# A linear-attention layer feeding a routed expert layer on one core: fourth and fifth chunk routed sooner, early fetches at once, breaks between indirect DMAs

## The chip, the cores and the metric

One core of one Trainium2 chip runs the whole kernel. The metric is device time in microseconds (us) for one execution. Three runs of the kernel before took 639.36, 640.45 and 640.35 us; their median is 640.35 us. The profile is of one further execution.

## The reference

Attention over B = 4 batches, H = 8 heads, S = 768 positions, head width D = 48: per position `state = f * state + outer(k, v)` with `f = sigmoid(f_logit)`, and `y = q @ state`. The result is laid out as x with N = 3072 rows of 384. Then a noisy top-2 router sends every row to two of eight experts:

```python
logits = x @ w_gate
noise_scale = np.log1p(np.exp(x @ w_noise))
noisy_logits = logits + noise_scale * noise
top2 = np.argpartition(-noisy_logits, 2, axis=1)[:, :2]
...
h = np.maximum(x[mask] @ w1[e], 0.0)
out[mask] += top2_w[mask, k, None] * (h @ w2[e])
```

`w1[e]` is 384 x 1024 and `w2[e]` is 1024 x 384; `top2_w` is the softmax of the two winning logits.

## The kernel before, in words

**Attention.** The 768 positions are six chunks of 128 (`NCH = 6`, `HALF = 3`). A chunk of all four batches is worked through in two groups, so there are twelve groups (`NG = 12`); groups 2c and 2c+1 make chunk c. A group turns q and k into transposed form on TensorE (L563), multiplies them (`scores`, `sc`, L584), masks the product on VectorE (`A`, L587), multiplies it with v (L615) and adds the share of the older state (L621). The state is carried on by GpSimd (`mid`, `st`, L604 and L606). The output yT is turned back for storing (`xp`, L632) and multiplied with the router's weights (`lt`, L642, and `lp`, L651).

**The order.** Everything up to the end of the attention is written out by hand: a loop over i runs the generators `back(i)` and `front(i)` (L1642 to L1689), and each name they yield ("sc0", "y1", "f" and so on) is a slot. In a slot the loop gives the router one step (three once the fifth chunk is being routed), lets at most one waiting scatter go (`puts.pop(0)()`), and gives one step to `first_loads` (L1517). After slot "L0" (or "f" in the groups without one) of every second i the next chunk's `route(c)` is started. In each engine's queue instructions run in the order in which they are written.

**Routing.** `route(c)` (L659) takes a chunk's logits to noisy logits, finds the two best (L681, L682), the gates (L686 to L694), counts per expert (L699 to L711), ranks the rows by two products on TensorE (`rk`, L716 and L717) and from these computes each row's place in its expert's list (`sloti`, L727). Then eight `put` steps each issue one indirect DMA on GpSimd (L731) that scatters 32-byte entries into the DRAM table `lists`. Behind each stands a memset (L739): one element of `spacer`, or, in the first three chunks at every third put, one row of 2048 elements of `spare`, which is a part of `hs_a`. This long memset is called a break below.

**Early pairs.** A pair is 256 rows of one expert. When three chunks are in the lists (24 puts), `first_loads` waits eight slots, fetches the row numbers of pairs 0 and 1 (`slots<-lists`, L864, issued by SyncE, SP), and gathers their x rows with four indirect DMAs on GpSimd (`xg<-x_rows`, L878). At the end of the attention they are turned on TensorE (`xgp`, L930) and give items 0 and 1, 256 rows each of two experts: first layer L983, second layer L1255. The eight puts of each later chunk stand behind the gathers, with a `spacer` each. When all six chunks are in the lists the remaining pairs are fetched, gathered and multiplied (L1145, L1311), and outputs are scattered onto the result by GpSimd (L1192).

Of the kernel before, what the change touches and what calls it, by code (L numbers as in the profile page):

```python
# [11 lines left out]
F32 = mybir.dt.float32  # L12
# [320 lines left out]
def kernel(  # L333
# [38 lines left out]
    nc = tc.nc  # L372
    B, H, S, D = q.shape
    N, DM = out.shape
# [3 lines left out]
    NCH = S // C  # L378
# [6 lines left out]
    HALF = NCH // 2  # L385
    NP = 3 * E
    NI = 2 * E
    NE = 2
# [270 lines left out]
    def route(c):  # L659
# [48 lines left out]
        else:  # L708
# [1 line left out]
        upto[c] = t([E, B + 1], "upto")  # L710
        nc.vector.tensor_tensor_scan(upto[c].rearrange("t e b -> t (e b)"), data0=carry.rearrange("t e b -> t (e b)"),  # L711
                                     data1=each.rearrange("t e b -> t (e b)"), initial=0.0, op0=ALU.mult, op1=ALU.add)
        for _ in range((4, 5, 5, 5, 8, 8)[c]):
            yield from pause()
        rk = one_bank(f"rk_{c}")[:, 0:B * E].rearrange("t (e b) -> t e b", b=B)
        nc.tensor.matmul(rk, lhsT=earlier, rhs=each[:, :, 1:], start=True, stop=False)  # L716
# [12 lines left out]
        def put(b, r):  # L729
            n_put.append(c)  # L730
            into = nc.gpsimd.indirect_dma_start(  # L731
                out=lists, out_offset=bass.IndirectOffsetOnAxis(ap=sloti[:, r, b:b + 1], axis=0),
                in_=entry[:, c, b, r, :], in_offset=None)
            tc.declare_no_dep(into.ins, group="lists", reason="slots differ")
            tc.add_to_no_dep_group("lists", into.ins)
            if c >= HALF:
                tc.declare_no_dep(into.ins, group="full", reason="slots differ")
                tc.add_to_no_dep_group("later", into.ins)
            nc.gpsimd.memset(spare[0:1, :] if c < HALF and len(n_put) % 3 == 0 else spacer, 0.0)  # L739

        puts.extend([partial(put, b, r) for b in range(B) for r in range(2)])
        yield


    steer_q = []

# [125 lines left out]

    def gather(p, halves=(0, 1)):

        if 0 in halves:
            xg[p] = moved.tile([128, 2, DM], F32, tag="xg", name=f"xg{p}", bufs=4)
        for s in halves:
            nc.gpsimd.indirect_dma_start(out=xg[p][:, s, :], out_offset=None, in_=x_rows[0:HALF * B * C] if p < NE else x_rows,  # L878
                                         in_offset=bass.IndirectOffsetOnAxis(ap=slots[p][:, s, 0:1], axis=0))

    def stored(p):
        if in_blocks(p):
# [634 lines left out]
    def first_loads():  # L1517
        while n_routed < HALF or len(n_put) < HALF * B * 2:
            yield
        for _ in range(8):  # L1520
            yield
        for what, p, pause in (("fetch", 2, 4), ("first", 0, 0), ("second", 0, 2), ("first", 1, 0), ("second", 1, 2), ("fetch", 3, 0)):
            if what == "fetch":
                ahead(what, p)
            elif what == "first":
                gather(p, (0,))
            elif what == "second":
                gather(p, (1,))
                done["gather"] = p + 1
            for _ in range(pause):  # L1530
                yield

    def tables():
# [12 lines left out]
    def through(g):  # L1546
        return 0 <= g < NG

    def front(i):
        if through(i + 1):  # L1550
            for s in range(2):
                turn_q(i + 1, s)
                yield f"q{s}"
            if i >= 0:
                load("q", i + 3)
                load("k", i + 3)
            for s in range(2):
                turn_k(i + 1, s)
                yield f"k{s}"
        if i == NG - 1:  # L1560
            turned_logits(i - 1)
            logits(i)
            features(i)
            turned_logits(i)
            yield "L0"
            yield "x0"
            yield "x1"
        else:
            yield "x0"
            if through(i):  # L1570
                features(i)
            yield "x1"
            if through(i - 1):
                turned_logits(i - 1)
        if i == -1:
            forget(1)
        elif through(i + 2):
            for s in range(2):
                summed(i + 2, s)
                yield f"L{s}"  # L1580
            ends(i + 2)
            if i == -2:
                for nm, g in (("f", 2), ("v", 1), ("q", 2), ("k", 2)):
                    load(nm, g)
            load("f", i + 5)
        if i == -3 or i > 2:
            forget(i + 3, halves if i < 0 else whole)
        yield "f"

    def back(i):  # L1590
# [39 lines left out]
        if i == -1:  # L1630
            scaled(0, halves)
        if through(i):
            yield "y1"
            for s in range(2):
                if i:
                    before(i, s, old)
                yield f"st{s}"
# [4 lines left out]
    for i in range(-3, NG):  # L1642
        for what in chain(back(i), front(i)):
# [16 lines left out]
                part_of_weights(n_part // 8, 1 + n_part // 4 % 2, n_part % 4)  # L1660
            elif i == NG - 1 and what in ("x0", "x1", "f"):
                zeros(4)
            for _ in range(6 if n_routed == NCH else 3 if n_routed == NCH - 1 else 1):
                next(router, None)
            slot += 1
            if puts and (what in ("q1", "x1", "L1", "sc1", "lg", "y1") + ("k1", "ds") * (n_routed == HALF) if n_routed < NCH - 1 else True) and not (done["fetch"] and not done["gather"]):
                puts.pop(0)()
            next(first_pairs, None)
            if i == NG - 1 and what == "st1":
# [3 lines left out]
            if what in fill.get(i, ()):  # L1673
# [4 lines left out]
                if what == "f":  # L1678
                    for _ in range(6):
                        next(router, None)  # L1680
            if what == ("L0" if through(i + 2) or i == NG - 1 else "f") and (i >= 2 and i % 2 == 0 or i == NG - 1):
                c = (i - 1) // 2
                router = chain(router, route(c))
                n_routed = c + 1
# [96 lines left out]
```

## Time and profile before

| what | value |
|---|---|
| median of three runs | 640.35 us |
| profiled execution, its own time | 634.29 us |
| span in that profile | 632.6 us |
| mean granted TensorE clock | 0.982 of full speed |
| TensorE matmul busy | 606.6 us, 96% |
| VectorE, ScalarE, GpSimd busy | 459.8, 279.8, 238.6 us |

The profiled execution took 6.06 us less than the median of the three runs, and its span lies 1.7 us below its own time. Times below are from the span's start. Attention ends at about 157 us; items 0 and 1 run to some 190 us, and the later items fill the rest. A granted clock of 1.00 is the full 2.4 GHz, 0.50 is 1.2 GHz.

### The profile page before, as it was taken

To read this page: it belongs to the slowest core of one execution; us is meant where nothing else is said; L and a number is where in the kernel's file an instruction comes from. 1 tells how busy PE (TensorE), PEld (TensorE's weight loads), DVE (VectorE), ACT (ScalarE), POOL (GpSimd) and SP (SyncE) were. 2 spreads that over 40 slices of the span, in tenths; PEclk is the share of its full clock that TensorE was granted. 3 is DMA by queue.
4 is the path that set the end of the run, shared out by engine and by line. 5 is a ranking of instruction groups with operands and counts; after the bars stand their busy time and mean duration, and the time that the engine had idled before them with its cause. 6 is when DMAs were issued, how large, how long until landed. Compare 5 with 4: busy or idle time off the path is not lost.

```text
span 632.6 us, 12895 instructions
## 1 busy us (share of the span) xinstructions
PE 606.6 (96%) x4767; PEld 543.4 (86%) x4767; DVE 459.8 (73%) x1031; ACT 279.8 (44%) x715; POOL 238.6 (38%) x250
## 2 busy tenths in 40 slices
PE   8999999878979999999999999999999999999995
PEld 7888878666969899998899899889888988898995
DVE  6658877745656675897797888787777978887850
ACT  5766665612113332327524731662175137316621
POOL 3213598861854513160134314322431262232032
PEclk9999999996989999999999999999999999999998
DMA  9999998885334667859576976688587849541024
GB/s 195 187 201 195 215 220 194 209 255 184 129 98 131 143 145 177 204 91 276 144 180 137 281 188 145 165 240 188 142 258 162 206 105 285 175 68 23 0 26 55
DMA packets 184511, 104.71 MB, mean 166 GB/s; under 512 B 144284, under 2 KB 177564, under 8 KB 184440
## 3 DMA queue, kind: packets, MB, share of 16 engines
q1 hardware_dynamic: 172392, 84.46, 52.3%
q0 software_dynamic: 12048, 19.35, 16.8%
q8 instruction: 39, 0.64, 0.4%
q14 instruction: 32, 0.26, 0.1%
HBM read 76.80 MB, written 27.23 MB: 164 GB/s over the span
## 4 chain that ended last, share of the span: by engine, by line
PE 88%; DVE 5%; issue 3%; another core or an unknown queue 2%; ACT 1%; DMA 1%; POOL 0%; POOLq 0%; DVEq 0%; ACTq 0%
PE y L1311 28%; PE D L1145 6%; PE E L1145 6%; PE C L1145 5%; PE B L1145 5%; PE sc L615 4%; PE sc L584 4%; PE hp L983 3%; PE y L1255 2%; PE L L541 2%; PE qp L563 2%; PE kp L563 2%; PE sc L621 2%; PE ds L596 2%
## 5 line engine op out<-in xcount | busy, mean ns | idle before, releaser
L1192 POOL DMA_INDIRECT out_dram<-ys,slots x48 | 79.7, 1661 | 192.2 <-DVE ys L1317 128.0
L1311 PE MATMUL y<-q_all,f_all 128*128 128x192 f32 x528 | 94.8, 327 | 0.8 <-ACT ys L1327 0.8
L1311 PEld LDWEIGHTS y<-q_all,f_all 128*128 128x128 f32 x528 | 86.6, 190 | 1.6 <-ACT ys L1327 1.3
L878 POOL DMA_INDIRECT xg<-x_rows,slots x48 | 52.2, 1087 | 71.5 <-DMA slots<-lists 28.2
L1311 PE MATMUL y<-w,hs_b 128*128 128x192 f32 x352 | 64.4, 326 | 0.0
L731 POOL DMA_INDIRECT lists<-entry,sloti x48 | 49.7, 1036 | 32.0 <-DVE sp L675 12.7
L1311 PEld LDWEIGHTS y<-w,hs_b 128*128 128x128 f32 x352 | 58.4, 190 | 0.4
L1317 DVE SCALAR_TENSOR_TENSOR ys<-y,slots,ys 128x192 f32<-128x192 f32 x66 | 27.4, 415 | 43.0 <-PE y L1311 16.5
L1153 ACT ACTIVATE hs_b<-hs_b 128x256 f32<-128x256 f32 x120 | 50.2, 418 | 8.5 <-DVE hs_b L1157 6.6
L1360 ACT ACTIVATE ys<-y,slots 128x192 f32<-128x192 f32 x22 | 9.2, 420 | 100.8 <-PE y L1311 100.8
L587 DVE TENSOR_TENSOR A<-sc,causal 128x1024 f32<-128x1024 f32 x24 | 28.6, 1220 | 16.9 <-PE sc L584 11.4
L584 PEld LDWEIGHTS sc<-qT,kT 64*128 64x128 f32 x384 | 24.3, 199 | 13.2 <-issue 8.4
L584 PE MATMUL sc<-qT,kT 64*128 64x128 f32 x384 | 27.3, 292 | 6.9 <-issue 3.8
L1311 PE MATMUL y<-w,f_all 128*128 128x192 f32 x176 | 32.7, 329 | 0.0
L1311 PE MATMUL y<-q_all,hs_b 128*128 128x192 f32 x176 | 32.7, 329 | 0.0
L1311 PEld LDWEIGHTS y<-q_all,hs_b 128*128 128x128 f32 x176 | 28.9, 190 | 2.1 <-issue 2.1
L1180 DVE TENSOR_TENSOR f_all<-hs_b 128x512 f32<-128x512 f32 x44 | 29.9, 684 | 0.0
L1311 PEld LDWEIGHTS y<-w,f_all 128*128 128x128 f32 x176 | 28.9, 190 | 0.8
L615 PEld LDWEIGHTS sc<-A,v_all 128*64 128x64 f32 x384 | 22.6, 144 | 7.4 <-issue 3.8
L1145 PE MATMUL C<-v_all,ws_b 128*128 128x256 f32 x96 | 28.7, 380 | 0.1
L615 PE MATMUL sc<-A,v_all 128*64 128x128 f32 x384 | 26.9, 289 | 1.5 <-issue 1.2
L1150 ACT COPY hs_a<-D 128x256 f32<-128x256 f32 x66 | 24.4, 370 | 7.2 <-PE D L1145 5.4
(274 smaller groups left out, 1410.5 us busy)
## 6 DMA issues: line engine op xcount, KB each, us to landing
w<-in_moe_w_dram SPq DMA_DIRECT2D x40, 384.0 KB
w_q<-in_moe_w_dram SPq DMA_DIRECT2D x10, 1536.0 KB
w<-in_moe_w_dram SPq DMA_DIRECT2D x6, 1536.0 KB
rows_of<-xg SPq DMA_DIRECT2D x18, 384.0 KB
v_all<-in_v_dram SPq DMA_DIRECT2D x12, 384.0 KB
x_rows<-xs SPq DMA_DIRECT2D x12, 384.0 KB
out_dram<-zero SPq DMA_DIRECT2D x24, 192.0 KB
k_all<-rows_of SPq DMA_DIRECT2D x48, 96.0 KB
```

Of the source, the lines that this page charges most:

```text
L563: nc.tensor.transpose(to[:, cols(hp)], flat[:, cols(hp)], ident)
L584: nc.tensor.matmul(sc[:, par, cols(hp)], lhsT=kT[g][rows(par), s, cols(hp)], rhs=qT[g][rows(par), s, cols(hp)], start=True, stop=True)
L587: nc.vector.tensor_tensor(A[g, s].rearrange("j r (a i) -> j (r a) i", i=C), sc.rearrange("j r (a i) -> j (r a) i", i=C), causal.unsqueeze( ...
L615: nc.tensor.matmul(at(g, s, h), lhsT=slot_of("v", g)[:, s, h, :], rhs=A[g, s][:, h % 2, cols(h // 2)], start=(j < 2), stop=(g < 2 and j >= ...
L731: into = nc.gpsimd.indirect_dma_start(out=lists, out_offset=bass.IndirectOffsetOnAxis(ap=sloti[:, r, b:b + 1], axis=0), in_=entry[:, c, b, ...
L878: nc.gpsimd.indirect_dma_start(out=xg[p][:, s, :], out_offset=None, in_=x_rows[0:HALF * B * C] if p < NE else x_rows, in_offset=bass.Indir ...
L1145: nc.tensor.matmul(banks[name, j], lhsT=half_of(x, k)[:, j * 128:(j + 1) * 128], rhs=half_of(y, k), start=first, stop=True, skip_group_che ...
L1153: nc.scalar.activation(at(to, j), at(y, j), AF.Relu, scale=-1.0 if more[0][0] == "-" else 1.0)
L1180: nc.vector.tensor_tensor(sm[which], x, y, op)
L1192: into = nc.gpsimd.indirect_dma_start(out=out, out_offset=bass.IndirectOffsetOnAxis(ap=slots[p][:, s, 2:3], axis=0), in_=ys[s], in_offset= ...
L1311: nc.tensor.matmul(to, lhsT=x[:, o, :], rhs=y[:, o, :], start=(start and o == 0), stop=(o == FH - 1), skip_group_check=not start)
L1317: nc.vector.scalar_tensor_tensor(to, in0=bank, scalar=gate[s], in1=to, op0=ALU.mult, op1=ALU.add)
```

## The change

The pauses in `route` and the steps per slot are altered, so that the fourth and the fifth chunk's places are known earlier; the fifth chunk's routing starts at "y1" of i = 10, and the logits it needs are moved ahead of that. `first_loads` waits two slots in place of eight, and then until four puts of the fourth chunk are out. Puts may now go in any slot once the fourth chunk is being routed. A new function `breath` counts indirect DMAs in a row, puts and early gathers alike, and makes every third one's memset a break: the old one for the first 24 puts, and after that two memsets in a row, of 768 and 576 elements, on one row of a tile (`xg[2]`) that is not in use yet. The sixth chunk's eight puts keep the spacer.

```diff
-        for _ in range((4, 5, 5, 5, 8, 8)[c]):
+        for _ in range((4, 5, 5, 17, 11, 8)[c]):
             yield from pause()
...
-            nc.gpsimd.memset(spare[0:1, :] if c < HALF and len(n_put) % 3 == 0 else spacer, 0.0)
+            breath(c <= HALF + 1)
...
+    in_a_row = [0]
+
+    def breath(broken):
+        in_a_row[0] = (in_a_row[0] + 1) % 3
+        if in_a_row[0] or not broken:
+            nc.gpsimd.memset(spacer, 0.0)
+        elif len(n_put) <= HALF * B * 2:
+            nc.gpsimd.memset(spare[0:1, :], 0.0)
+        else:
+            if NE not in xg:
+                xg[NE] = moved.tile([128, 2, DM], F32, tag="xg", name=f"xg{NE}", bufs=4)
+            flat = xg[NE].rearrange("p s w -> p (s w)")
+            nc.gpsimd.memset(flat[0:1, :], 0.0)
+            nc.gpsimd.memset(flat[0:1, 0:DM + DM // 2], 0.0)
...
-        if 0 in halves:
+        if 0 in halves and p not in xg:
...
+            if p < NE:
+                breath(True)
...
-        for _ in range(8):
+        for _ in range(2):
             yield
...
+            while what == "fetch" and p == NE and len(n_put) < HALF * B * 2 + 4:
                 yield
...
-            if through(i - 1):
+            if through(i - 1) and i != NG - 2:
                 turned_logits(i - 1)
...
+            if i == NG - 2:
+                turned_logits(i - 1)
             yield "y1"
...
-            for _ in range(6 if n_routed == NCH else 3 if n_routed == NCH - 1 else 1):
+            for _ in range(6 if n_routed == NCH else 2 if n_routed == HALF + 1 else 3 if n_routed == NCH - 1 and i == NG - 1 else 1):
...
-            if puts and (what in ("q1", "x1", "L1", "sc1", "lg", "y1") + ("k1", "ds") * (n_routed == HALF) if n_routed < NCH - 1 else True) and not (done["fetch"] and not done["gather"]):
+            if puts and (what in ("q1", "x1", "L1", "sc1", "lg", "y1") + ("k1", "ds") * (n_routed == HALF) if n_routed <= HALF else True) and not (len(n_put) >= HALF * B * 2 and not done["fetch"]):
                 puts.pop(0)()
...
-            if what == ("L0" if through(i + 2) or i == NG - 1 else "f") and (i >= 2 and i % 2 == 0 or i == NG - 1):
+            if what == ("L0" if through(i + 2) or i == NG - 1 else "y1") and (i >= 2 and i % 2 == 0 or i == NG - 1):
```

**GpSimd, from the last carried state (`st`) on.** The numbers at the ends of names are buffer numbers; `sloti_1996` before and `sloti_1951` after hold the fourth chunk's places. Before:

```order
L606 TENSOR_TENSOR st_1816<-mid_1817,ending 128x384
L878 DMA xg_1933<-x_rows,slots_1894 128x384 x2
L878 DMA xg_1951<-x_rows,slots_1896 128x384 x2
L731 DMA lists<-entry,sloti_1996 24832x8
L739 MEMSET spacer 1x1
L731 DMA lists<-entry,sloti_1996 24832x8
L739 MEMSET spacer 1x1
```

After:

```order
L606 TENSOR_TENSOR st_1828<-mid_1829,ending 128x384
L731 DMA lists<-entry,sloti_1951 24832x8
L750 MEMSET spacer 1x1
L731 DMA lists<-entry,sloti_1951 24832x8
L750 MEMSET spacer 1x1
L731 DMA lists<-entry,sloti_1951 24832x8
L757 MEMSET xg_1964 1x768
L758 MEMSET xg_1964 1x576
L731 DMA lists<-entry,sloti_1951 24832x8
L750 MEMSET spacer 1x1
L893 DMA xg_1980<-x_rows,slots_1805 128x384
L750 MEMSET spacer 1x1
```

The four gathers stood back to back, with the fourth chunk's puts behind them and nothing but spacers between. Now three puts go first, and a break (L757, L758) follows the third, sixth and ninth indirect DMA and so on. Further down, the fifth chunk's eight puts follow at once with breaks behind the third and the sixth counted so, six late breaks in all, and the sixth chunk's eight have spacers alone.

**TensorE, from group 9's `xp` to group 10's products.** Before:

```order
L632 MATMUL xp_1920<-ident,yT_1865 128x128 x8
L651 MATMUL lp_1936<-ident,lgs_1829 128x128 x2
L541 MATMUL L_0_1943<-f_all,causal 128x384
L541 MATMUL L_1_1947<-f_all,causal 128x384
L584 MATMUL sc_0_1955<-qT_1880,kT_1898 128x128 x8
L716 MATMUL rk_1966<-each_1914,earlier 128x32
L717 MATMUL rk_1966<-upto_1918,ones 128x32
L584 MATMUL sc_1_1969<-qT_1880,kT_1898 128x128 x8
L642 MATMUL lt_1987<-yT_1865,w_lg 32x256 x4
L615 MATMUL sc_0_1955<-A_0_1964,v_all 64x128 x8
```

After:

```order
L632 MATMUL xp_1920<-ident,yT_1884 128x128 x8
L716 MATMUL rk_1933<-each_1861,earlier 128x32
L717 MATMUL rk_1933<-upto_1874,ones 128x32
L651 MATMUL lp_1936<-ident,lgs_1843 128x128 x2
L541 MATMUL L_0_1943<-f_all,causal 128x384
L541 MATMUL L_1_1956<-f_all,causal 128x384
L584 MATMUL sc_0_1967<-qT_1895,kT_1908 128x128 x8
L584 MATMUL sc_1_1986<-qT_1895,kT_1908 128x128 x8
L642 MATMUL lt_2003<-yT_1884,w_lg 32x256 x4
L615 MATMUL sc_0_1967<-A_0_1976,v_all 64x128 x8
```

The fourth chunk's ranking (`rk`) has moved from between group 10's two score products to a place ahead of them, behind group 9's `xp`. In the same manner the fifth chunk's ranking has moved from behind the last `lp` to between the two halves of group 11's L621, which is not shown.

**SyncE's DMA queue, around the early fetch.** Before:

```order
L546 DMA p_end<-P_1744 1x768
L550 DMA ending<-p_end 48x8x1 x2
L636 DMA x_rows<-xs_1726 128x2x384
L912 DMA w_0_135<-in_moe_w_dram 128x2x384
L523 DMA v_all<-in_v_dram 128x16x48
L912 DMA w_0_135<-in_moe_w_dram 128x2x384
L864 DMA slots_1894<-lists 128x2x4
L864 DMA slots_1896<-lists 128x2x4
```

After:

```order
L546 DMA p_end<-P_1744 1x768
L879 DMA slots_1805<-lists 128x2x4
L879 DMA slots_1807<-lists 128x2x4
L550 DMA ending<-p_end 48x8x1 x2
L636 DMA x_rows<-xs_1726 128x2x384
L929 DMA w_0_135<-in_moe_w_dram 128x2x384
L523 DMA v_all<-in_v_dram 128x16x48
L929 DMA w_0_135<-in_moe_w_dram 128x2x384 x3
```

The two fetches of row numbers stood behind two `ending`, an x row store, a part of the first expert's weights and the last `v_all`; now they stand ahead of these.

## Rows read from the trace of the kernel before

**Rows 1.** The page of before: busy time by engine; the closing chain by engine.
```profile
PE 606.6 (96%) x4767; PEld 543.4 (86%) x4767; DVE 459.8 (73%) x1031; ACT 279.8 (44%) x715; POOL 238.6 (38%) x250
...
PE 88%; DVE 5%; issue 3%; another core or an unknown queue 2%; ACT 1%; DMA 1%; POOL 0%; POOLq 0%; DVEq 0%; ACTq 0%
```

**Rows 2.** Chain of waits, 120 to 190 us: start, us, what held it.
```profile
127.39 0.34 PE rk L716 x2
127.73 0.22 PE rk L717 x2
...
135.47 0.22 PE lp L651 x2
135.69 3.83 issue
...
142.75 5.45 another core or an unknown queue
...
171.01 4.97 another core or an unknown queue
```

**Rows 3.** TensorE in time: start, us, line, out<-in, count, [idle before <-releaser].
```profile
126.23 1.16 PE L584 MATMUL sc<-qT,kT 64*128 64x128 f32 x16 [0.84 <-DVE kT L578]
...
129.54 1.97 PE L615 MATMUL sc<-A,v_all 128*64 128x128 f32 x32
...
139.52 2.08 PE L584 MATMUL sc<-qT,kT 64*128 64x128 f32 x16 [3.83 <-issue]
...
149.50 3.64 PE L615 MATMUL sc<-A,v_all 128*64 128x128 f32 x32 [0.31 <-DVE A L587]
...
171.24 1.47 PE L1255 MATMUL y<-q_all,hs_a 128*128 128x192 f32 x8
172.54 1.46 PE L1255 MATMUL y<-q_all,f_all 128*128 128x192 f32 x8
...
177.21 2.93 PE L1255 MATMUL y<-q_all,f_all 128*128 128x192 f32 x8 [2.88 <-DVE f_all L1180]
```

**Rows 4.** Windows: bounds, length, busy and count by engine, PE clock, DMA, GB/s.
```profile
38.67:60.47 21.80, 21.80 (x337) 18.12 (x333) 16.41 (x35) 14.55 (x33) 6.11 (x6) 1.00 1.00 203
71.69:120.19 48.50, 47.03 (x679) 38.29 (x675) 39.69 (x95) 29.71 (x65) 43.23 (x51) 1.00 0.99 213
126.23:132.46 6.23, 6.23 (x108) 5.18 (x109) 5.35 (x11) 0.82 (x3) 1.60 (x2) 1.00 0.87 236
135.69:154.09 18.40, 11.01 (x104) 8.31 (x105) 6.73 (x27) 2.47 (x9) 8.52 (x17) 0.63 0.83 272
174.33:183.77 9.44, 5.98 (x24) 5.39 (x24) 3.58 (x14) 0.46 (x2) 5.38 (x10) 0.82 0.06 4
```

**Rows 5.** GpSimd (POOL) in time, 69 to 190 us.
```profile
75.85 1.79 POOL L739 MEMSET hs_a<- 1x2048 f32 x1
...
125.09 0.83 POOL L606 TENSOR_TENSOR st<-mid,ending 128x384 f32<-128x384 f32 x1
130.56 1.51 POOL L878 DMA_INDIRECT xg<-x_rows,slots  x1 [4.64 <-DMA slots<-lists]
...
145.02 0.95 POOL L731 DMA_INDIRECT lists<-entry,sloti  x1 [0.22 <-issue]
...
158.78 0.96 POOL L731 DMA_INDIRECT lists<-entry,sloti  x1 [12.73 <-DVE sp L675]
...
170.30 0.96 POOL L731 DMA_INDIRECT lists<-entry,sloti  x1 [0.23 <-issue]
...
179.55 0.96 POOL L731 DMA_INDIRECT lists<-entry,sloti  x1 [0.23 <-issue]
```

**Rows 6.** VectorE (DVE) in time: one small copy twice.
```profile
75.81 1.87 DVE L707 COPY each<-upto 128x8 f32<-128x8 f32 x1
...
100.82 0.16 DVE L707 COPY each<-upto 128x8 f32<-128x8 f32 x1
```

**Rows 7.** The page of before, DMA queues: fetches of instructions.
```profile
q8 instruction: 39, 0.64, 0.4%
```

More of the change, by code (lines that the diff above doesn't have):

```diff
@@ L1530, in first_loads @@
             for _ in range(pause):
+                yield
+            while what == "fetch" and p == NE and len(n_put) < HALF * B * 2 + 4:
                 yield
```

## The prediction

> **What bounds the kernel now.** I read the page first, for the engine that carries the time. TensorE is busy for 606.6 us of 632.6, and 88% of the chain that ended last is TensorE's own work, so time can only come from places where TensorE stands idle or runs slowly [rows 1]. The other entries of that chain are small, but two of them are unusual: "issue" at 3%, and "another core or an unknown queue" at 2%, which on a single core means that the trace shows no work to wait for. Next I followed the chain in time to see where these sit. Three pieces stand out: 3.83 us at 135.69, 5.45 us at 142.75 and 4.97 us at 171.01 [rows 2]. TensorE's timeline shows the same places from its side, and that work just behind them takes twice as long as before them [rows 3]. Then I cut windows, because a share of the whole span says nothing about a place of 18 us. Last I read GpSimd over the same stretch, because the change rebuilds its queue.
>
> **The first slow place.** From 126.23 to 132.46 group 10 does its two score products, the ranking, lt, L615 and L621 in 6.23 us at a granted clock of 1.00 [rows 4]. Without the ranking's 0.34 + 0.22 us [rows 2] that is 5.67 us. From 135.69 to 154.09 group 11 does the same work in 18.40 us at a clock of 0.63 [rows 4]. The excess is 12.7 us. It has two parts: idle time, and then the lower of the two clock levels, which came after the idle time. The score products of sixteen took 2.08 against 1.16 us, and L615 3.64 against 1.97 us [rows 3].
>
> **The second slow place.** From 174.33 to 183.77 TensorE does three second-layer products of eight and little else, in 9.44 us at a clock of 0.82 [rows 4]. One such product takes 1.30 us when nothing disturbs it (starts 171.24 and 172.54), so three take 3.9 us, and the one at 177.21 took 2.93 us instead of 1.46 [rows 3]. The excess is 5.5 us. Together the two places hold 12.7 + 5.5 = 18.2 us.
>
> **What GpSimd does there.** From 130.56 to 146 it issues twelve indirect DMAs, four gathers and eight puts, at some 1.3 us each with gaps of 0.2 to 0.3 us; from 158.78 to 180.5 it issues sixteen more. From 146 to 158.78 it has nothing to do [rows 5]. TensorE's first idle time begins 5 us into the first run, the chain gets going again at 148.2, two us after that run's end, and the third hole opens 12 us into the second run. In the earlier half, where a break of 1.79 us stands behind every third put [rows 5], no such hole is seen: in four groups' work from 71.69 to 120.19 TensorE is idle for 1.47 us in all (48.50 less 47.03), at a clock of 1.00 [rows 4]. I read this so: while indirect DMAs are issued one behind another, notices between the other engines come late, and a break lets them through. The trace shows the coincidence, not the mechanism.
>
> **The sum, gains.** If the breaks work, both excesses go: 18.2 us. There may be 0.8 us more: at 126.23 TensorE waited 0.84 us for kT [rows 3], which stood on VectorE behind the fourth chunk's gates; these now come a group sooner. I leave this out and keep it for the low end.
>
> **The sum, costs.** (1) A run with breaks is not free. The undisturbed pace is 21.80 us for two groups, 43.6 for four; the stretch with puts took 48.50 [rows 4]. That is 4.9 us more, less two rankings (0.56 each) 3.8, for the 21 puts that begin inside it: 0.18 us each. The late run has four gathers and sixteen puts before the last break, so 20 x 0.18 = 3.6 us. But the late break is shorter. By the old one's pace, 1.79 us for 2048 elements [rows 5], 768 + 576 elements take 1.18 us, with two starts some 1.3 us. Two thirds of the length could let through less, so I take 5 us, between 3.6 and the 12.7 us that a run with no effective break cost. (2) The sixth chunk's eight puts have no breaks, and two of the fifth chunk's stand unbroken before them: ten in a row. In the second run the ninth put began at 170.30 and the hole opened at 171.01 [rows 2, 5]. The bounds are therefore 0 and the 5.5 us of the second place; Ten puts at 1.26 us end 12.6 us after they began, just where that hole opened, so I take 1.5. (3) New waits in queue order: the two rankings now stand before `lp` and inside L621, and TensorE would wait there if VectorE's counts were late. `sloti` likewise stands ahead of group 10's mask. The trace does not show such a wait; the nearest rows are TensorE's waits for VectorE, 0.84 us for kT and 2.88 us for f_all [rows 3], so the bounds are 0 and 2.88. The logits come from the group before, which is nearer to the first, so I take 1. (4) GpSimd's own time: six breaks of 1.3 us are 8 us more. It is idle from 125.92 to 130.56 and from 146 to 158.78 [rows 5], 17 us together, and it stands on the chain with 0% [rows 1], so this costs nothing. Without that cover the early gathers would be late for `xgp` at the attention's end; they would have to slip from some 140 to over 150 us. (5) SyncE's queue: a fetch that waits for the 24th put now holds the x row store, part of the first weights and the last `v_all` behind it. The slots had landed by 130.56 [rows 5], and the last `v_all` is first read by L615 at 149.50 [rows 3], so there are 19 us for it: nothing.
>
> Against the breaks speaks VectorE. A copy of 8 elements a row took 1.87 us beside a break at 75.85, and 0.16 us elsewhere [rows 5, 6]: it was held until the memset ended. The Trainium skill ("SBUF — State Buffer", section "Who interferes with whom") states the rule behind this: GpSimd and VectorE share a pair of ports, copies, casts and tensor_scalar can take both, and the one that comes second is blocked wholly. By that rule alone six breaks could hold VectorE for 8 us, and the gain would shrink from 10.5 to under 3 us; the trace agrees that the block is whole. I price it from the rows: VectorE's instructions of that kind beside the late breaks are a few small copies off the chain and the two kT copies, so at most two are hit on the path, and this lies inside the 5 us of (1), whose 0.18 us a put was measured with such hits in it.
>
> Sum: 18.2 - 5 - 1.5 - 1 = 10.7, taken as 10.5 us. The profiled execution's own time is 634.29 us, so its like would be 623.8. The median of the runs lies 6.06 us above it; 640.35 - 10.5 gives 629.9 us, which is my forecast on the scale of the runs.
>
> **Rivals.**
>
> *The late breaks are too short or too few.* They are 1.3 us, the ones known to work 1.79. If the first place stays as long as it is and the second shrinks to nothing, 5.5 less 1.6 of costs are saved: 636.4 us. For it: nothing in the trace shows that 1.3 us is enough. Against it: short idle times of a few tenths do not help, yet the old breaks help every time, so the threshold lies somewhere in between. Chance 0.20.
>
> *The holes have another cause and only move.* TensorE's notices could be late for fetches of instructions (39 packets in the whole run [rows 7]) or for weights loading at 272 GB/s [rows 4]. For it: the first place has the highest rate in my windows. Against it: the second place has 4 GB/s [rows 4] and the same kind of hole, and 39 packets are few. Gains and costs then nearly cancel: 640.4 us, within 1.3 us either way. Chance 0.07.
>
> *Slower: one more hole.* If breaks of this length do not release anything, GpSimd now issues without a real pause from 126 on, where it used to stand idle to 130.56 [rows 5]. Group 10's clean 6.23 us [rows 4] then gets a hole of its own, of the size of the third, 4.97 us [rows 2], while the later ones stay: 640.35 + 5 = 645.3 us. It decides from the point where a break no longer lets the notices through within 5 us of the run's start. Chance 0.09.
>
> **How the numbers follow.** The forecast has 0.64. Within it the largest saving is 18.2 + 0.8 - 3.6 = 15.4 us (625), and with (1) at 8, (2) at 5.5 and (3) at 1 it saves 3.7 (636.7). With the first rival's 636.4 and a little for its own spread the range is 624 to 638 us, which leaves out the other two rivals with 0.16 and the tails. A measurement of this kernel can tell some 0.2%, 1.3 us. The forecast and the first rival lie on the faster side by more than that, 0.64 + 0.20 = 0.84; no change has 0.07, slower 0.09.
>
> **What would show it.** Right: group 11's stretch from its first score product to the end of L621 near 6 to 9 us at a granted clock near 1.00; the chain without pieces of 4 us between 130 and 185; the breaks at about 1.3 us between the gathers; the early gathers before 145. The price of (2) would show as a hole near the end of the sixth chunk's puts, between 165 and 175. Wrong: a clock of 0.5 to 0.6 in group 11 again (first rival), holes of the same length while no indirect DMA is issued (second), or group 10 at over 10 us (third). If the attention's end comes 12 us sooner, yet the total does not, something behind it is waiting for work that did not move, and the sum fails at its last step.

## The result, and the profile after

The changed kernel took 621.79 us (median of six runs, 618.89 to 626.94), the kernel before 638.93 us (six runs, 635.83 to 640.45). The ratio is 0.974, 95% interval 0.969 to 0.979: faster by 17.1 us by the medians. The forecast was 10.5 us and its range ended at 624, so the sign was right and the size was not. The profiled execution is the fastest of the six, 618.89 us with a span of 617.1, 15.5 us less than the span before.

The page of the changed kernel: busy time by engine, the granted clock in 40 slices, and the fetches of instructions.

```profile
PE 598.7 (97%) x4767; PEld 536.9 (87%) x4767; DVE 460.7 (75%) x1031; ACT 279.7 (45%) x715; POOL 248.3 (40%) x260
...
PEclk9999999999999999999999999999999999999998
...
q8 instruction: 39, 0.64, 0.4%
```

TensorE works 7.9 us less for the same 4767 products [rows 1] and the clock stays at its upper level in all slices but the last. GpSimd works some 10 us more. The fetches of instructions are what they were [rows 7].

Windows of the changed kernel, columns as in [rows 4]: group 10 to the end of group 11; group 11 alone; the first layer of items 0 and 1 and their second layer up to the place of the old second hole; the three products that stood in that hole.

```profile
124.91:141.60 16.69, 15.88 (x240) 12.72 (x239) 12.53 (x37) 5.87 (x16) 14.48 (x23) 1.00 0.90 240
135.12:141.60 6.48, 6.48 (x109) 5.16 (x109) 4.77 (x21) 1.27 (x4) 5.75 (x10) 1.00 0.89 239
141.60:165.13 23.53, 23.53 (x145) 21.67 (x144) 18.84 (x69) 7.05 (x17) 20.30 (x33) 1.00 0.71 254
161.22:165.13 3.91, 3.91 (x27) 3.91 (x26) 3.14 (x10) 0.96 (x2) 3.26 (x7) 1.00 0.03 3
```

Group 11 from its first score product to the end of L621 takes 6.48 us at a clock of 1.00, and 7.03 us with the 0.55 us of waiting ahead of it; before, with the 3.83 us of waiting ahead of it, it took 18.40 us at 0.63 [rows 3, 4]. The three products take 3.91 us, where the same three took 9.44 us at 0.82 [rows 4]. Both excesses of the prediction, 12.7 and 5.5 us, are gone.

TensorE in time, changed kernel; these rows answer to [rows 3].

```profile
124.91 2.06 PE L584 MATMUL sc<-qT,kT 64*128 64x128 f32 x32
...
135.12 2.06 PE L584 MATMUL sc<-qT,kT 64*128 64x128 f32 x32 [0.55 <-issue]
...
137.68 2.15 PE L615 MATMUL sc<-A,v_all 128*64 128x128 f32 x32
...
161.22 1.47 PE L1272 MATMUL y<-q_all,f_all 128*128 128x192 f32 x8
...
179.88 0.52 PE L947 MATMUL xgp<-ident,xg 128*128 128x128 f32 x3 [1.32 <-DMA xg<-x_rows,slots]
```

The score products of both halves take 2.06 us together, without a wait between them, and group 10's (the first row) no longer wait for kT. The last row is new: TensorE waits 1.32 us for the gather of pair 2's rows, which was not waited for before.

GpSimd in time, changed kernel: a put with its break, the first put after the last break, the last put, and the first gather of pair 2.

```profile
129.27 1.09 POOL L731 DMA_INDIRECT lists<-entry,sloti  x1 [0.21 <-issue]
130.36 0.73 POOL L757 MEMSET xg<- 1x768 f32 x1
131.15 0.57 POOL L758 MEMSET xg<- 1x576 f32 x1
...
157.86 0.96 POOL L731 DMA_INDIRECT lists<-entry,sloti  x1 [0.17 <-issue]
...
170.36 0.96 POOL L731 DMA_INDIRECT lists<-entry,sloti  x1 [0.22 <-issue]
...
175.32 1.01 POOL L893 DMA_INDIRECT xg<-x_rows,slots  x1 [0.30 <-issue]
```

The break is 0.73 + 0.57 us. From its start to the next put it takes 1.52 us (130.36 to 131.88), where a spacer takes 0.30, so GpSimd loses some 1.2 us each time, 7.3 us in all. Ten puts from 157.86 to 171.3 stand unbroken, and in this execution nothing is held up beside them. From 126.68 to 171.3 GpSimd has no pause above 0.3 us. Behind that stand one scatter of outputs, which takes 3.33 us, and then the gathers of pair 2, for which TensorE waits 1.32 us. In c1 and j4 below the same scatter takes 1.62 us, so not all of that wait need be the breaks'.

### The profile page after: what moved, and what is told of

Read it like the earlier page. It is cut to its first block, busy times and chain, and to the rows that moved or that the text cites. A ratio compares the mean times of both kernels' runs of the same rounds, so it can differ in the third digit from the quotient of the medians.

```text
span 617.1 us, 12902 instructions
## 1 busy us (share of the span) xinstructions
PE 598.7 (97%) x4767; PEld 536.9 (87%) x4767; DVE 460.7 (75%) x1031; ACT 279.7 (45%) x715; POOL 248.3 (40%) x260
## 4 chain that ended last, share of the span: by engine, by line
PE 86%; POOL 4%; issue 2%; DVE 2%; DMA 2%; ACT 2%; POOLq 0%; DVEq 0%; ACTq 0%
PE y L1328 31%; PE E L1162 7%; PE D L1162 7%; PE C L1162 5%; PE B L1162 5%; PE sc L615 4%; PE sc L584 3%; POOL lists L731 3%; PE L L541 2%; PE qp L563 2%; PE sc L621 2%; PE kp L563 2%; PE A L1162 2%; PE P L1025 2%; PE ds L596 2%
## 5 line engine op out<-in xcount | busy, mean ns | idle before, releaser
L1209 POOL DMA_INDIRECT out_dram<-ys,slots x48 | 81.8, 1704 | 194.1 <-DVE ys L1334 136.5
L893 POOL DMA_INDIRECT xg<-x_rows,slots x48 | 50.7, 1056 | 68.4 <-DMA slots<-lists 25.6
L584 PEld LDWEIGHTS sc<-qT,kT 64*128 64x128 f32 x384 | 22.5, 188 | 6.9 <-issue 3.1
L615 PEld LDWEIGHTS sc<-A,v_all 128*64 128x64 f32 x384 | 21.1, 136 | 6.9 <-issue 3.1
L615 PE MATMUL sc<-A,v_all 128*64 128x128 f32 x384 | 25.6, 277 | 1.0 <-issue 0.9
L584 PE MATMUL sc<-qT,kT 64*128 64x128 f32 x384 | 24.9, 279 | 1.1 <-issue 0.5
```

The source lines that it names most:

```text
L584: nc.tensor.matmul(sc[:, par, cols(hp)], lhsT=kT[g][rows(par), s, cols(hp)], rhs=qT[g][rows(par), s, cols(hp)], start=True, stop=True)
L615: nc.tensor.matmul(at(g, s, h), lhsT=slot_of("v", g)[:, s, h, :], rhs=A[g, s][:, h % 2, cols(h // 2)], start=(j < 2), stop=(g < 2 and j >= ...
L1209: into = nc.gpsimd.indirect_dma_start(out=out, out_offset=bass.IndirectOffsetOnAxis(ap=slots[p][:, s, 2:3], axis=0), in_=ys[s], in_offset= ...
```

## The experiments

The runs come from five series of measurements (the recorded expectations say call for series). The kernels of one series ran on one chip with the kernel before beside them, and ratios are to that. A fact found on the way has to be told first, since all readings depend on it: in three series the kernel before took 611.6 to 613.0 us, and in two 642.8 us (in the first measurement 638.9). Times of different series are therefore not compared, only ratios. A hole is a time in which TensorE stands idle beside a run of indirect DMAs, as in the two places of the prediction. I call the two sorts *series with holes* and *series without*.

| run | series' kernel before, us | median, us | ratio | 95% interval |
|---|---|---|---|---|
| e1, no late breaks | 642.8 | 640.7 | 0.997 | 0.993 to 1.001 |
| e2, before with late breaks | 642.8 | 629.6 | 0.981 | 0.975 to 0.986 |
| e3, breaks in sixth chunk too | 642.8 | 629.6 | 0.981 | 0.976 to 0.987 |
| e4, half breaks | 642.8 | 632.3 | 0.984 | 0.979 to 0.989 |
| g1, before | 642.8 | 639.7 | 0.998 | 0.994 to 1.003 |
| g2, change | 642.8 | 628.4 | 0.978 | 0.972 to 0.984 |
| g3, before without first breaks | 642.8 | 651.6 | 1.015 | 1.008 to 1.021 |
| g4, sixth break dropped | 642.8 | 626.0 | 0.975 | 0.970 to 0.981 |
| c1, change | 613.0 | 616.6 | 1.004 | 1.001 to 1.008 |
| f1, breaks doubled | 613.0 | 626.1 | 1.022 | 1.018 to 1.026 |
| f2, before without first breaks | 613.0 | 615.7 | 1.001 | 0.997 to 1.005 |
| f3, sixth break dropped | 613.0 | 611.9 | 1.001 | 0.997 to 1.004 |
| j1, every second | 611.6 | 621.2 | 1.014 | 1.011 to 1.018 |
| j2, every fourth | 611.6 | 617.1 | 1.004 | 1.000 to 1.008 |
| j3, every sixth | 611.6 | 613.4 | 1.001 | 0.998 to 1.004 |
| j4, no late breaks | 611.6 | 612.0 | 1.001 | 0.998 to 1.005 |
| k1, every sixth | 612.5 | 614.1 | 1.002 | 0.998 to 1.006 |
| k2, every second | 612.5 | 619.6 | 1.012 | 1.006 to 1.019 |

### Breaks or order: e1 and e2

My theory was that breaks let held-back notices through; the rival, that the new order alone (earlier ranking, gathers spread among puts) did it. e1 keeps the order and takes the breaks:

```diff
-        if in_a_row[0] or not broken:
+        if in_a_row[0] or not broken or len(n_put) > HALF * B * 2:
```

> The changed kernel with everything moved as in it, but the six late breaks are one-element spacers. If the breaks do the work, the holes of before come back in group 11 or just behind the attention: a granted clock near 0.6 there and a ratio to the kernel before of 0.99 to 1.01. If the new order alone (rankings sooner, gathers spread among the puts) does it, the ratio stays near 0.974.

Measured 0.997: nothing is left of the gain. TensorE in e1:

```profile
145.34 1.97 PE L563 MATMUL kp<-ident,k_all 128*128 128x128 f32 x8 [4.69 <-issue]
...
150.20 3.79 PE L584 MATMUL sc<-qT,kT 64*128 64x128 f32 x32
...
172.63 0.61 PE L716 MATMUL rk<-each,earlier 128*128 128x32 f32 x2 [3.62 <-DVE each L707]
```

The holes are back, at other instructions: 4.69 us before group 11's keys are turned, score products at nearly twice the time (3.79 us for 32, against 2.06), and 3.62 us before the last ranking. e2 does the reverse: `breath` is put into the kernel before, behind its gathers and puts, and nothing is moved.

```diff
-            nc.gpsimd.memset(spare[0:1, :] if c < HALF and len(n_put) % 3 == 0 else spacer, 0.0)
+            breath(c <= HALF + 1)
...
+            if p < NE:
+                breath(True)
```

> The kernel before with a break after every third of its gathers and of the fourth and fifth chunk's puts, and nothing moved: five or six breaks. If the breaks do the work, most of the 17 us come: ratio 0.975 to 0.982, holes at 135 and at 142 gone. The hole at 171 may stay, since there the fifth chunk's puts run into the sixth's. If the order does it, ratio 0.99 to 1.01.

Measured 0.981, 12.5 us: the breaks alone bring most of the gain. In e2's trace group 11's 32 score products take 2.06 us again, and the wait that is left is for pair 2's gather:

```profile
142.10 2.06 PE L584 MATMUL sc<-qT,kT 64*128 64x128 f32 x32 [0.32 <-DVE kT L578]
...
188.93 0.52 PE L947 MATMUL xgp<-ident,xg 128*128 128x128 f32 x3 [1.95 <-DMA xg<-x_rows,slots]
```

What the order adds to the breaks is not settled: 0.974 and 0.978 for the change stand against 0.981, and the intervals overlap.

### How long a break, and where else: e4 and e3

e4 leaves out the first of the two memsets, so a break is 0.57 us.

> The changed kernel with only the second memset of each late break, 576 elements, about 0.57 us instead of 1.3. If the length has to be near 1.3 us, part of the holes return: 627 to 636. If any pause of over half a microsecond lets the notices through, 618 to 622.

The ratio is 0.984, and TensorE's rows show why:

```profile
142.51 1.97 PE L563 MATMUL kp<-ident,k_all 128*128 128x128 f32 x8 [2.76 <-issue]
146.88 1.97 PE L632 MATMUL xp<-ident,yT 128*128 128x128 f32 x8 [2.41 <-ACT yT L625]
...
168.80 0.38 PE L716 MATMUL rk<-each,earlier 128*128 128x32 f32 x2 [1.59 <-issue]
```

Holes of 2.76, 2.41 and 1.59 us remain, and e4 still gains 10 us, so a break need not let everything through to be worth something; in this trace 0.57 us was not enough for all of it. e3 gives the sixth chunk's puts breaks as well (`breath(True)` in `put`).

> The changed kernel, and breaks in the sixth chunk's eight puts as well. If ten unbroken puts in a row still cost something in some executions (those at 624 to 627), the median falls to about 619 and the spread narrows. If they are too few for a hole, the two or three more breaks make the last early outputs and gathers 3 us later, and the time is the same or up to 3 us longer.

It came out at 0.981, slower than the change's 0.974 and 0.978 by the middle values, though not beyond their intervals; the spread did not narrow. In its trace TensorE waits 5.47 us for pair 2's gather:

```profile
188.33 0.87 PE L947 MATMUL xgp<-ident,xg 128*128 128x128 f32 x3 [5.47 <-DMA xg<-x_rows,slots]
```

How much of this is the price of the further breaks is not shown, since f2 below has a wait of the same length there without any break.

### The same kernels where nothing is held up: c1, f1, f2, f3

The second series was meant to price a break. c1 is the changed kernel itself.

> The changed kernel itself, unaltered, beside the others of this call. Ratio to the kernel before 0.97 to 0.98, as first measured; its trace tells how much of group 11 and of the wait for pair 2's gather repeats.

It missed: 1.004, slower than the kernel before, which took 613.0 us here. f2 is the kernel before with the memset of the first three chunks made a spacer everywhere.

```diff
-            nc.gpsimd.memset(spare[0:1, :] if c < HALF and len(n_put) % 3 == 0 else spacer, 0.0)
+            nc.gpsimd.memset(spacer, 0.0)
```

> The kernel before with one-element spacers in place of all eight breaks of the first three chunks, nothing else. If runs of indirect DMAs hold up the others wherever they stand, holes open between 75 and 125 us as well: 10 to 25 us slower than the kernel before, clock below 0.9 there. If it takes what only the late place has (gathers, weights arriving), the time is within 3 us of the kernel before or up to 4 us better, since the breaks go.

It too came out level, 1.001, and its trace has no break anywhere. TensorE in f2, group 11's score products, one of the three products of the old second hole, and pair 2:

```profile
130.70 2.06 PE L584 MATMUL sc<-qT,kT 64*128 64x128 f32 x32 [0.32 <-DVE kT L578]
...
158.42 1.47 PE L1255 MATMUL y<-q_all,f_all 128*128 128x192 f32 x8
...
181.25 0.90 PE L930 MATMUL xgp<-ident,xg 128*128 128x128 f32 x3 [5.48 <-DMA xg<-x_rows,slots]
```

All puts and the four early gathers stand unbroken, and from group 10 to 175 us there is no hole and no lower clock; TensorE waits there only for kT and for the early gathers themselves, 0.30 and 1.40 us. So in this series nothing was held up that breaks could release. What the late breaks cost the attention can be read from windows over groups 10 and 11, c1 first, then f1 below, whose breaks are twice as long:

```profile
123.27:139.07 15.80, 15.23 (x239) 12.44 (x238) 12.48 (x35) 6.12 (x16) 13.77 (x22) 1.00 0.67 181
```

```profile
127.92:143.73 15.81, 15.24 (x240) 12.44 (x239) 11.71 (x36) 6.12 (x16) 13.36 (x21) 1.00 0.88 242
```

That is nothing: j4, the same order without late breaks, takes 15.85 us there (its row is shown further down). Any cost of the breaks must lie behind that. TensorE in c1:

```profile
132.71 2.06 PE L584 MATMUL sc<-qT,kT 64*128 64x128 f32 x32 [0.57 <-DVE mx L681]
...
181.24 0.87 PE L947 MATMUL xgp<-ident,xg 128*128 128x128 f32 x3 [5.20 <-DMA xg<-x_rows,slots]
```

```profile
177.28 1.01 POOL L893 DMA_INDIRECT xg<-x_rows,slots  x1 [3.75 <-DMA slots<-lists]
```

Pair 2's gathers begin at 177.28, after the row numbers have come from `lists`, and TensorE waits 5.20 us for them. By itself this row does not price the breaks, since f2 waits 5.48 us at the same place with none; no trace of the kernel before was taken in a series without holes. f1 repeats the two memsets, so each break is twice as long.

> The changed kernel with each late break done twice, four memsets, about 2.7 us. If a break itself costs TensorE time in the attention (0.18 us and more for each put, VectorE blocked for 1.3 us more, six times), group 10 and 11 grow by 2 to 4 us. If its only price is GpSimd's time, those two stay at 6.5 to 7 us each, and the 6 x 1.4 = 8 us show as one longer wait for pair 2's gathers (1.32 us in the changed kernel), total 5 to 8 us above the changed kernel.

It took 9.5 us more than c1 by the medians, and the wait is the same one, 3.2 us longer:

```profile
190.32 0.87 PE L948 MATMUL xgp<-ident,xg 128*128 128x128 f32 x3 [8.36 <-DMA xg<-x_rows,slots]
```

That is a third of the difference. The profiled execution of f1 also lost 3.0 us against c1's in the four early groups (49.26 us for 46.22), ahead of every late break, behind a wait of 1.32 us for VectorE and at a clock of 0.97.

f3 drops the break behind the fifth chunk's sixth put.

```diff
-            breath(c <= HALF + 1)
+            breath(c <= HALF + 1 and len(n_put) < (HALF + 2) * B * 2 - 2)
```

> The changed kernel without its last late break, the one behind the fifth chunk's sixth put, so thirteen puts stand unbroken. If GpSimd's chain up to pair 2's gathers is what is left to gain, that wait goes and the time falls by about 1.3 us. If thirteen in a row open a hole as in the second run of the kernel before, it is 3 to 6 us longer.

1.001 against c1's 1.004, with intervals that overlap; in its trace the wait for pair 2 is 0.79 us.

```profile
177.64 0.52 PE L947 MATMUL xgp<-ident,xg 128*128 128x128 f32 x3 [0.79 <-DMA xg<-x_rows,slots]
```

### The two sorts side by side: g1 to g4

> The kernel before, unaltered, for a trace beside the others of this call; the ratio has to be 1.00. In the first call of experiments the kernel before took 642.8 us on one chip, in the second 613.0 on another, where no kernel showed a hole, with or without breaks. If the holes belong to some chips and not to the kernel, this one either takes about 640 us with holes near 135 to 150 and at 170, or about 613 with none, and the other three follow it.

> The changed kernel, unaltered. Where the kernel before has holes, ratio 0.97 to 0.98; where it has none, 1.000 to 1.008, since only the breaks' price is left. Rival: the second call's 1.0044 came from something that differed between the calls but not with the holes, then the ratio is free of what the kernel before shows.

> The kernel before without its eight first breaks. Where the kernel before has holes, there are more of them, between 75 and 125 us, and it is 10 to 25 us slower than the kernel before; where it has none, within 0.5% of it, as in the second call (1.0005).

> The changed kernel without its last late break. On a chip without holes 3 us faster than the changed kernel (second call: 1.0005 against 1.0044), since GpSimd reaches pair 2's gathers sooner. On a chip with holes thirteen unbroken puts either open one late hole, 3 to 6 us slower than the changed kernel, or 1 to 3 us faster.

This was a series with holes, and all four followed, g3 by less than expected (8.8 us by the medians, for 10 to 25). g1's TensorE rows are like those of [rows 3]:

```profile
140.53 1.57 PE L584 MATMUL sc<-qT,kT 64*128 64x128 f32 x16 [2.46 <-issue]
143.67 2.08 PE L584 MATMUL sc<-qT,kT 64*128 64x128 f32 x16 [1.57 <-issue]
...
180.04 2.93 PE L1255 MATMUL y<-q_all,f_all 128*128 128x192 f32 x8 [4.32 <-issue]
```

g2 gave 0.978, g3 was slower than the kernel before by 1.5%, and g4 gave 0.975. The trace of g2 is of the slowest of its six executions, 634.78 us, and shows that the changed kernel can still have a hole, at the end of its ten unbroken puts (the last ends at 178.97):

```profile
181.32 8.24 PE L1000 MATMUL hp<-xt_a,w 128*128 128x256 f32 x24 [3.35 <-DVE xt_a L948]
```

The same 24 products take 5.34 us in the first trace of the changed kernel. The clearest pair is g3 and f2, the same kernel in the two sorts of series. Windows over the same four groups that [rows 4] has from 71.69 to 120.19, f2 first:

```profile
71.39:116.81 45.42, 44.99 (x678) 37.69 (x675) 37.56 (x87) 29.34 (x65) 33.33 (x56) 1.00 0.93 197
```

```profile
72.32:134.89 62.57, 53.03 (x679) 42.95 (x675) 37.24 (x81) 29.82 (x65) 36.87 (x56) 0.89 0.81 179
```

The same products take 45.42 us at a clock of 1.00 in the one and 62.57 us at 0.89 in the other, while GpSimd is busy for 33.33 and 36.87 us with the same puts. So the first breaks do in the early place what the late ones do later, where there is something to release.

### More and fewer breaks: j1 to j4, k1, k2

These change the divisor of `breath` for the late breaks (2, 4 and 6 for 3); j4 is e1's kernel.

> The changed kernel with a late break behind every second indirect DMA in place of every third: ten breaks for six. If breaks at every third still leave TensorE late in the attention (0.18 us for each put, as the prediction priced a broken run), groups 10 and 11 get 1 to 2 us shorter, but pair 2's gathers come 4 x 1.5 = 6 us later; total 2 to 5 us above the changed kernel. If nothing is left to gain, the full 6 us are lost, with or without holes in the kernel before.

> The changed kernel with five late breaks, behind every fourth. GpSimd gains 1.5 us. Where the kernel before has holes: 1 us faster to 2 us slower than the changed kernel. Where it has none: about 1.5 us faster than the changed kernel, ratio to before near 1.002.

> The changed kernel with three late breaks, behind every sixth, 7.7 us of issuing between two. Where the kernel before has holes: the first hole of before opened 5 us into its run, so part of them returns, 4 to 10 us above the changed kernel. Where it has none: 4 us faster than the changed kernel, ratio below 1.000.

> The changed kernel without late breaks, as in the first call (0.9972 where the kernel before took 642.8). If this call's kernel before has holes again, 0.99 to 1.005. If it takes about 613, this is the order alone without the breaks' price: 3 to 8 us faster than the kernel before, since the early fetch no longer waits behind other transfers.

> Three late breaks, behind every sixth indirect DMA, as once before (1.0011 where the kernel before took 611.6 us). If this call's kernel before takes about 640 us, it shows whether 7.7 us of unbroken issuing is short enough: ratio 0.975 to 0.98 if so, 0.982 to 0.995 if holes of part length open between the breaks. If it takes about 612, 1.001 again.

> Ten late breaks, behind every second indirect DMA (1.0141 where the kernel before took 611.6 us, 6 us above the changed kernel). If this call's kernel before takes about 640 us: 0.984 to 0.988 if breaks at every third already leave nothing to release, so that GpSimd's 6 us are lost in full; 0.97 to 0.978 if hold-ups are left at every third which more breaks take away, as the prediction's 0.18 us for each put has it.

Both series were without holes, so they price breaks and tell nothing about how few would do where there are holes; that stays open. Kernels with ten breaks took 1.2 to 1.4% more than the kernel before, with five 0.4%, with three 0.1 to 0.2%, with none 0.1%. Only the ten stand clear of none beyond the intervals. The expectation for j4, 3 to 8 us faster than before, missed: without breaks and without holes the new order is worth nothing that can be measured. j4's pair 2 shows the slack that breaks use up, GpSimd's gather first and then the TensorE row that needs it:

```profile
166.65 1.01 POOL L893 DMA_INDIRECT xg<-x_rows,slots  x1 [1.67 <-DMA slots<-lists]
```

```profile
176.80 0.49 PE L947 MATMUL xgp<-ident,xg 128*128 128x128 f32 x3
```

The gathers begin 10.2 us before they are needed. The changed kernel's six breaks take 7.3 us of GpSimd's time ahead of them. From the start of the first gather to the product that needs it 4.56 us pass there (175.32 to 179.88), so the slack is gone.

One execution each of f3 and j4 took 1588 us, more than twice the others. The profiles are of other executions and show nothing of it. The equal length suggests a definite cause, perhaps the kernel's general path, but no run tells it, and it should be looked into before either is used. No execution of the kernel before or of the changed kernel did this.

## Why the prediction was wrong in size

**What bounds, and both holes: right.** The forecast read the two places as 12.7 and 5.5 us of excess. Measured by the windows of the changed kernel, group 11 without its 0.56 us of ranking takes 5.92 us in place of 18.40, so 12.5 us, and the three products 3.91 in place of 9.44, so 5.5 us. e1 and e2 show that the breaks took them away.

**The step that failed is the sum's costs, 7.5 us, above all (1), 5 us for a run with breaks.** One window over the whole stretch, from group 10's first product (`qp`) to the start of the last second-layer products ahead of pair 2's, before and then changed:

```profile
120.19:194.56 74.37, 62.04 (x469) 52.51 (x466) 38.74 (x123) 18.29 (x43) 43.75 (x64) 0.89 0.58 176
```

```profile
120.09:175.80 55.71, 54.90 (x468) 47.36 (x465) 39.09 (x125) 18.46 (x43) 48.37 (x72) 1.00 0.61 183
```

It is 18.7 us shorter, where the gains counted came to 18.2 and the sum kept 10.7. So what (1) to (3) cost here was no more than what had been left out on the other side, such as the wait of 0.84 us for kT, which went, as the prediction had held possible.

What (1) measures is seen against j4, the change's order with no breaks and no holes. Group 10 to the end of group 11, then the items up to the same place as in the changed kernel:

```profile
124.14:139.99 15.85, 15.23 (x239) 12.44 (x238) 12.21 (x35) 6.12 (x16) 13.20 (x24) 1.00 0.75 202
139.99:163.53 23.54, 23.54 (x147) 21.67 (x144) 18.14 (x69) 6.89 (x16) 18.87 (x35) 1.00 0.87 289
```

Against these the changed kernel needs 16.69 for 15.85 us, 0.84 us more, and 23.53 for 23.54 us, nothing. And the 0.84 us are not the breaks' price, as c1 has the same breaks and takes 15.80. As I read it, they are hold-ups that were left between the breaks, and these vary: in other traces from series with holes the same instructions took 16.59 us (g4), 17.63 (e3) and, in the slowest execution of g2, 20.10, over 4 us more. So (1) was too high for the measured result, but an execution near it exists.

The forecast multiplied 0.18 us by twenty DMAs and rounded up to 5. That price was read where it could not be taken apart. c1 does the same four early groups with the same breaks in 46.22 us, f2 without any in 45.42. By these traces, of the 3.8 us charged there some 2.3 (48.50 less 46.22) go with the series with holes, 0.8 are the long breaks', and 0.7 come from a base of 43.6 us that two earlier groups made too short. Of the nine traces with these breaks from series without holes, seven lie at 45.8 to 46.2 us (f1 and j1 at 49.3 and 50.8, at a lower clock); the nine from the others lie at 48.4 to 53.6. And the price was charged for DMAs that stand beside the items' products, where the changed kernel lost no time against j4.

**(2), ten unbroken puts, 1.5 us: nothing** in the profiled execution; no hole stands beside them. That is in part luck: g2's trace has the hole, 3.35 us and then the lower clock, at the end of these puts, where the prediction said it would show. **(3), new queue waits, 1 us: 0.2 to 0.3 us.** Before group 11's first score product TensorE waits 0.55 us in the changed kernel, where f2, with the old order, waits 0.32; j4, with the new order, waits 0.62. The rankings have no wait of their own.

**(4), GpSimd's own time, "costs nothing": wrong, the other way.** I looked for cover only up to the early gathers. The queue is one: its 7.3 us of breaks also stand ahead of the next pairs' gathers, and j4's 10.2 us of slack there are gone in the changed kernel, which waits 1.32 us. How much the breaks cost by this in series without holes is not shown, as f2 has such a wait without them.

Behind the window above the changed kernel loses 3.3 us of its lead, so that 15.5 us are left between the two spans. 1.32 us are the wait for pair 2. Two waits in the later items come to 3.25 us, against some 1.4 us that the kernel before lost between 400 and 500 us in smaller waits:

```profile
325.11 0.70 PE L1162 MATMUL E<-v_all,k_all 128*128 128x256 f32 x2 [1.51 <-ACT hs_a L1167]
384.32 0.70 PE L1162 MATMUL E<-v_all,k_all 128*128 128x256 f32 x2 [1.74 <-ACT hs_a L1167]
```

The first trace of the kernel before has no such wait, but g1, the same kernel, has one of 1.83 us, and c1, the changed kernel, has none there above 0.6 us. So they are not shown to be the change's.

**The rivals.** Too-short breaks: e4 shows what it would have looked like, and 1.3 us was long enough for both places. One more hole in group 10: it took 6.83 us from 124.91 to 131.74 in the changed kernel, so none. The rival on other causes is half right in a way I had not thought of: the holes do not only depend on the kernel. Fetches of instructions are not the cause that decides, as the page counts 39 of them with holes and without. In the series without holes that had the changed kernel, it was slower than before by 0.4%, the sign to which I gave 0.09, but without the hole that this rival named.

**VectorE's block** cost groups 10 and 11 nothing that can be measured where nothing was held up, as c1's 15.80 us with breaks, f1's 15.81 with doubled ones and j4's 15.85 without show. By the rule of the Trainium skill alone ("SBUF — State Buffer", "Who interferes with whom") up to 8 us could have gone; the runs show that the late breaks met hardly anything on the path.

## What to carry to other kernels

Before pricing a wait, find an undisturbed run of the same instructions as the base; two other groups of the same loop were 0.7 us off in four, and most of the 3.8 us read there as the price of puts with breaks went away where nothing was held up. A pause put into a queue is paid by everything behind it in that queue, not only by what stands beside it, so follow the queue to the next instruction that another engine waits for. Where a gain comes from taking away waits that the program does not ask for, measure both kernels in several series: here the same change is worth 2.2 to 2.6% in two and costs 0.4% in another. Of the versions run, the change without its last break (0.975 and 1.001) has the best middle values over both, though within the intervals of its neighbours, and apart from its one unexplained execution.

## What was not expected of the hardware

The kernel before took 638.9 to 642.8 us in three series of measurements and 611.6 to 613.0 us in three others. Within a series it was steady: 609.2 to 621.1 us over 29 executions in one, 635.4 to 648.9 over 17 in another. The difference is the holes: TensorE idle for 2 to 5 us at a time, then at the lower clock, while GpSimd issues indirect DMAs one behind another. GpSimd's issuing itself is as fast in both sorts, 0.96 us a put. What sets a series' sort is open; the runs list the same chip number once with holes and once without, so that number does not tell it, and no experiment here could choose the sort.

Where there are holes, a pause of 1.3 us after every third indirect DMA prevented them in the first trace of the changed kernel, and one of 0.57 us did so only in part. In g2's trace waits of 1.99 and 2.37 us about group 10 and the 3.35 us behind the ten unbroken puts are left. That it works by letting delayed notices through is still my reading: no row of the trace shows a notice on its way. Nor was a pause of another kind than a memset tried.
